# Sliding-window attention and a gated feed-forward layer: seven block products for eight in the last six tiles, with attention placed in the output stage

## The chip, the cores and the metric

The kernel runs on one core of one Trainium2 chip. Five engines of the core work from queues of their own, each in order: TensorE (PE; its weight loads are shown as PEld), VectorE (DVE), ScalarE (ACT), GpSimd (POOL) and SyncE (SP). They meet at semaphores. Results of TensorE land in PSUM, eight banks of 128 x 512 float32. The metric is the device time of one execution in microseconds.

## The reference

For each of 8 batches and 8 heads, queries, keys and values are 576 x 64. A query sees itself and the 63 keys before it:

```python
scores = scale * np.matmul(q, k.transpose(0, 1, 3, 2))
mask = (rel >= 0) & (rel < window)          # window = 64, rel = query - key
attn = softmax(np.where(mask, scores, -1e9))
x = (attn @ v).transpose(0, 2, 1, 3).reshape(B * S, H * D)     # 4608 tokens x 512
gate = np.maximum(x @ w_gate, 0.0)          # w_gate, w_val: 512 x 1536
val = x @ w_val
return (gate * val) @ w_out                 # w_out: 1536 x 512
```

## The kernel before

The 4608 tokens are cut into ten tiles: tiles 0 to 3 of 384 tokens (TT) and tiles 4 to 9 of 512 (WT), the wide ones. NS is 4. Matrix operands are float16, sums float32.

*Feed-forward part of a tile.* In the hidden stage (`hidden`, line 450 and on) the 1536 hidden features are 12 blocks of 128 (f), and the 512 inputs are 4 chunks of 128. For each f, four matmuls (L481) make the gate block in a PSUM bank, ScalarE applies the ReLU into `r_sb` (L466), four matmuls make the value block in another bank, and VectorE multiplies it by `r_sb` into `g_sb` (L469). The 12 `g_sb` blocks feed the output stage (`output`, `out_mm`, L495): for each 128 tokens, 12 matmuls of 512 columns, an evacuation by ScalarE (L502) and a DMA from SP.

*Attention of a tile.* q and k of a batch are loaded by DMA from the POOL queue (`qk_load`, L167) and transposed by VectorE in four instructions of 128 x 576 (`qk_trans`, L185). v is loaded by POOL's queue (`v_load`, L191) and partly copied to other partitions by POOL (`v_spread`, L200 and L202). A wide tile has two quads of four windows of 64 queries. For a quad, TensorE writes scores into four banks (`q_st`, L236), ScalarE takes the exponential (L365) and VectorE multiplies by the band mask (L369). Then TensorE multiplies by v (`t_pv`, L384), VectorE takes reciprocals of the sums (L399), normalises (L404) and transposes into `xt` (L409), the input of the hidden stage. Tiles 0 to 3 do the same in units of 192 tokens (L270, L275, L296, L310, L320, L340). While one tile is in its hidden and output stages, the attention of the next is placed among its matmuls.

*Order of the work.* The order in each queue is written by a planner, `Weaver`. Code that emits TensorE's main stream advances an estimated clock; other work is put into a heap with a due time (`W.at`) and is emitted, in order of due time, as soon as the clock passes it. Due times set only the order in each queue: an engine runs its next instruction when what it needs is there. `ahead(t)` plans at the beginning of tile t: for a wide tile the next tile's attention (`plan_wide`: scores, exponentials and masks, values) and k, q and v of the tile after that (`wide_loads`). A tile buffer drawn anew from a pool with n buffers waits until every use of the buffer n draws ago is over.

*Buffers.* PSUM is split into four single banks (`f_ps`, hidden and output stages, and a rest of the values) and two double banks (`a_ps`, scores and values). k and q landing buffers (`a_in`) are double.

Of the kernel before, what the change touches and what calls it, by code (L numbers as in the profile page):

```python
# [13 lines left out]
MUL = mybir.AluOpType.mult  # L14
ONE_ONE = struct.unpack("<f", struct.pack("<I", 0x3C003C00))[0]
# [29 lines left out]
def kernel(  # L45
# [20 lines left out]
    G = 4  # L66
# [11 lines left out]
    a_in = ctx.enter_context(tc.tile_pool(name="a_in", bufs=2))  # L78
    a_p = ctx.enter_context(tc.tile_pool(name="a_p", bufs=12))
    a_n = ctx.enter_context(tc.tile_pool(name="a_n", bufs=2))  # L80
    x_sb = ctx.enter_context(tc.tile_pool(name="x_sb", bufs=3))
    g_sb_p = ctx.enter_context(tc.tile_pool(name="g_sb", bufs=2))
    f_sb = ctx.enter_context(tc.tile_pool(name="f_sb", bufs=3))
    f_ps = ctx.enter_context(tc.tile_pool(name="f_ps", bufs=4, space=bass.MemoryType.PSUM))
    a_ps = ctx.enter_context(tc.tile_pool(name="a_ps", bufs=2, space=bass.MemoryType.PSUM))
# [3 lines left out]
    wo = persist.tile([128, NF, DM], FP16)  # L89
    qTs = [persist.tile([128, 2, S, 2], FP16, name=f"qT{i}") for i in range(2)]  # L90
# [72 lines left out]
    def qk_load(b, name, hh):  # L163

        tile_ = nat[b, name, hh] = a_in.tile([128, S // 32 * D], FP16, name=f"{name}{hh}", bufs=2)
        src = (q if name == "q" else k)[b, G * hh:G * hh + G]
        nc.gpsimd.dma_start(tile_, src.rearrange("h (i j) d -> (h i) (j d)", i=32))  # L167

    def first_load(name):

        t32 = nat["32", name] = x_sb.tile([128, S // 32 * D], FP32, name=f"{name}32", bufs=1)
        nc.sync.dma_start(t32, (q if name == "q" else k)[0, 0:G].rearrange("h (i j) d -> (h i) (j d)", i=32))

    def first_round(name, copies):
        n = S // 32 * D // len(copies)
        to = nat[0, name, 0] = a_in.tile([128, S // 32 * D], FP16, name=f"{name}0", bufs=2)
# [40 lines left out]
    def one_bank(name):  # L217
        return f_ps.tile([128, 512], FP32, name=name, tag="h")

    def two_banks(name):  # L220
        return a_ps.tile([128, 2, 512], FP32, name=name, tag="a")

    def st_tiles(u):
        d = units.setdefault(u, {})
        if u == 0:
            d["st"] = [one_bank("st") for _ in range(G)]
        else:
            halves = [two_banks("st") for _ in range(2)]
            d["st"] = [halves[g // 2][:, g % 2] for g in range(G)]
# [35 lines left out]
    def u_exp(u, i, hhs=(0, 1)):  # L265
        d = units[u]
        if d["p"][i] is None:
            d["p"][i] = a_p.tile([128, 2 * UB, 64], FP16, name="p")
# [10 lines left out]
    def u_pv(u, hhs=(0, 1), banks=None):  # L279

        d = units[u]
        if "pv" not in d:
            if banks:
                d["pv"] = [one_bank("pv") for _ in range(2)]
            else:
                both = two_banks("pv")
# [62 lines left out]
    wides = {}  # L349

# [3 lines left out]
    def q_st(qd):  # L354

        halves = [two_banks("st") for _ in range(2)]
        d = quads[qd] = {"st": [halves[g // 2][:, g % 2] for g in range(G)], "p": [None] * G}
# [4 lines left out]
    def q_exp(qd, g):  # L362
        d = quads[qd]
        d["p"][g] = a_p.tile([128, 2 * QW, 64], FP16, name="pw")
        nc.scalar.activation(d["p"][g].rearrange("p n c -> p (n c)"), d["st"][g], ACT.Exp, scale=scale)  # L365

    def q_mask(qd, g):
        p = quads[qd]["p"][g]
        nc.vector.tensor_tensor(p, p, mask[:, None, :].to_broadcast([128, 2 * QW, 64]), MUL)  # L369

    def t_pv(t):

        d = wides[t] = {"pv": [two_banks("pv") for _ in range(2)], "rest": one_bank("pv"),
                        "x": a_n.tile([128, 2, WS, 2, D // 2], FP16, name="xw"), "r": a_n.tile([128, 2, WS, 1], FP32, name="rw")}
        for qh in range(2):
            qd = 2 * (t - NS) + qh
            for hh in range(2):
                for i in range(QW):
                    b, vw = divmod(q_window(qd, i), NG)
                    for s in range(2):  # L380
                        n = 2 * (QW * qh + i) + s
                        to = d["pv"][hh][:, n // BS, VW * (n % BS):] if n < 2 * BS else d["rest"][:, VW * (2 * hh + n - 2 * BS):]
                        for j in range(G):
                            nc.tensor.matmul(to[32 * j:32 * j + 32, 0:D + 1],  # L384
                                             quads[qd]["p"][j][:, QW * hh + i, 32 * s:32 * s + 32],
                                             v16s[b % 2][:, vw, G * hh + j, 0:D + 1],
                                             start=True, stop=True, skip_group_check=True)
        return 1.25

    def t_parts(d, hh):  # L390

        rest = d["rest"][:, 0:4 * VW].rearrange("p (a s c) -> p a s c", a=2, c=VW)
        return [(d["pv"][hh][:, k, 0:BS * VW].rearrange("p (s c) -> p s c", c=VW), BS * k, BS * k + BS) for k in range(2)] + [
            (rest[:, hh], 2 * BS, WS)]

    def t_recip(t, hh):
        d = wides[t]
        for pv, s0, s1 in t_parts(d, hh):
            nc.vector.reciprocal(d["r"][:, hh, s0:s1], pv[:, :, D:D + 1])  # L399

    def t_norm(t, hh, k):
        d = wides[t]
        pv, s0, s1 = t_parts(d, hh)[k]
        nc.vector.tensor_tensor(d["x"][:, hh, s0:s1], pv[:, :, 0:D].rearrange("p s (c e) -> p s e c", e=2),  # L404
                                d["r"][:, hh, s0:s1, :, None].to_broadcast([128, s1 - s0, 2, D // 2]), MUL)

    def t_turn(t, hh):
        dst = xt_tile(t)[:, 2 * hh:2 * hh + 2].rearrange("p e (s c) -> p s e c", c=32)
        nc.vector.transpose(dst, wides[t]["x"][:, hh])  # L409
        if hh == 1:  # L410
            normed[0] = t

    def plan_wide(t, TA, TB, P):
        for qd, T in ((2 * (t - NS), TA), (2 * (t - NS) + 1, TB)):
            W.at(T, lambda qd=qd: q_st(qd))
            for g in range(G):
                W.at(T + 0.8 + 0.55 * g, lambda qd=qd, g=g: q_exp(qd, g))
                W.at(T + 1.35 + 0.55 * g, lambda qd=qd, g=g: q_mask(qd, g))
# [301 lines left out]
```

## Time and profile before

| quantity | value |
|---|---|
| three runs | 324.62 us each |
| span of the profiled execution | 323.2 us; its own time is not listed, so 1.4 us around it are taken from the runs |
| PE busy | 312.2 us, 97% |
| DVE busy | 191.7 us, 59% |
| ACT busy | 128.9 us, 40% |
| POOL busy | 95.2 us, 29% |
| granted TensorE clock | 1.000 |
| tile 2, from 68.06 us | 25.68 us |
| tile 3, from 93.74 us | 26.15 us |
| tile 4, from 119.89 us | 33.89 us |
| tiles 5 to 8 | 33.86 us each where shown |

Busy time on PE includes the modelled tail of each matmul, so its share does not tell how near TensorE is to its peak. The start of a matmul minus the start of the one before it is its price in a stream. Idle time of an engine that does not set the end costs nothing. In an answer of the profile, a line gives line number, engine, operation, output and inputs with their shapes, a count after x, and busy time with the mean of one; the idle time before it and what ended it stand at the end. In the chain and the timelines the first two numbers are start and length in us.

### The profile page before, as it was taken

The page shows a single profiled execution, that of the slowest core. Times are in us where ns is not written, and L with a number is a line of the kernel's source. Part 1 is how long each engine was busy: PE and PEld are TensorE (multiplying, and loading weights), DVE is VectorE, ACT ScalarE, POOL GpSimd, SP SyncE. Part 2 cuts the span into 40 slices and gives each one's busy share as a digit, 9 for nine tenths or more (in the row PEclk, how much of TensorE's full clock was granted, in tenths as well). Part 3 has the DMA queues.
Part 4 walks back from the last instruction along what each step waited for, and adds up shares of the span by engine and source line. Part 5 has one row for each costly group of instructions (what it writes and reads, how often), then busy time and mean ns, then how long its engine had stood idle before and what let it go on. Part 6 is the DMA issues. An engine that isn't in the chain of part 4 may idle for free.

```text
span 323.2 us, 8917 instructions
## 1 busy us (share of the span) xinstructions
PE 312.2 (97%) x3861; PEld 167.7 (52%) x3861; DVE 191.7 (59%) x367; ACT 128.9 (40%) x256; POOL 95.2 (29%) x140
## 2 busy tenths in 40 slices
PE   4689999999999999999999999999999999999996
PEld 2466958656556644454445444454445444544444
DVE  5937962677938759564765656673767145724410
ACT  3545325534434623542354234613371337223322
POOL 8759317284910290029100920072000000000000
PEclk9999999999999999999999999999999999999999
DMA  7999997979294079009910893092000200020002
GB/s 214 182 190 199 179 143 173 157 127 184 35 203 60 9 95 202 3 5 122 218 10 2 108 203 27 2 103 88 0 3 34 99 0 2 5 110 20 0 34 98
DMA packets 52488, 29.48 MB, mean 91 GB/s; under 512 B 38880, under 2 KB 43872, under 8 KB 52448
## 3 DMA queue, kind: packets, MB, share of 16 engines
q0 software_dynamic: 46688, 18.29, 48.8%
q1 hardware_dynamic: 5616, 10.55, 9.0%
q8 instruction: 30, 0.49, 0.6%
q14 instruction: 10, 0.08, 0.1%
q10 hardware_dynamic: 144, 0.07, 0.1%
HBM read 37.75 MB, written 9.44 MB: 146 GB/s over the span
## 4 chain that ended last, share of the span: by engine, by line
PE 94%; DMA 2%; POOL 1%; DVE 1%; issue 1%; ACT 0%; DVEq 0%; POOLq 0%
PE h L481 59%; PE op L495 28%; PE st L236 3%; PE pv L384 2%; DMA v<-in_v_dram 2%; PE pv L296 1%; PE op L527 1%; DVE x L320 0%; POOL v L191 0%; DVE v L202 0%; POOL k L167 0%; DVE v L200 0%; POOL q L167 0%; DVE xt L340 0%; POOL ident L107 0%
## 5 line engine op out<-in xcount | busy, mean ns | idle before, releaser
L469 DVE TENSOR_TENSOR g_sb<-r_sb,h 128x512 f16<-128x512 f32 (+1 forms) x120 | 75.4, 631 | 88.5 <-PE h L481 86.8
L481 PE MATMUL h<-xt,wg 128*128 128x512 f16 (+2 forms) x544 | 111.8, 335 | 1.5 <-issue 0.9
L481 PE MATMUL h<-xt,wv 128*128 128x512 f16 (+2 forms) x544 | 111.4, 335 | 0.0
L466 ACT ACTIVATE r_sb<-h 128x512 f32<-128x512 f32 (+1 forms) x120 | 66.8, 558 | 89.1 <-PE h L481 81.3
L495 PE MATMUL op<-wo,g_sb 128*128 128x512 f16 x420 | 93.8, 379 | 0.0
L481 PEld LDWEIGHTS <-wg 128*128 128x128 f16 x544 | 50.8, 98 | 43.9 <-issue 2.0
L481 PEld LDWEIGHTS <-wv 128*128 128x128 f16 x544 | 50.4, 98 | 40.9
L495 PEld LDWEIGHTS <-g_sb 128*128 128x128 f16 x420 | 40.4, 98 | 47.1
L191 POOL DMA_DIRECT2D v<-in_v_dram x41 | 34.6, 864 | 94.0 <-PE pv L384 89.2
L502 ACT COPY o_sb<-op 128x512 f32<-128x512 f32 x35 | 20.5, 586 | 85.9 <-PE op L495 85.2
L369 DVE TENSOR_TENSOR pw<-pw,mask 128x512 f16<-128x512 f16 x48 | 19.2, 422 | 14.6 <-ACT pw L365 14.3
L365 ACT ACTIVATE pw<-st 128x512 f16<-128x512 f32 x48 | 25.7, 605 | 5.0 <-PE st L236 4.5
L200 POOL COPY v<-v 64x512 f16<-64x512 f16 (+1 forms) x22 | 16.0, 728 | 27.1 <-DMA v<-in_v_dram 26.3
L185 DVE STREAM_TRANSPOSE kT<-k 128x576 f32<-128x576 f32 x16 | 20.0, 1247 | 0.1
L185 DVE STREAM_TRANSPOSE qT<-q 128x576 f32<-128x576 f32 x16 | 19.3, 1238 | 0.1
L202 POOL COPY v<-v 64x512 f16<-64x512 f16 (+1 forms) x22 | 17.0, 771 | 1.0
L404 DVE TENSOR_TENSOR xw<-pv,rw 128x448 f16<-128x448 f32 (+1 forms) x36 | 16.2, 507 | 0.4
L236 PEld LDWEIGHTS <-kT 32*128 32x128 f16 x1152 | 10.6, 92 | 9.3 <-issue 7.7
L270 ACT ACTIVATE p<-st 128x384 f16<-128x384 f32 (+1 forms) x40 | 13.8, 439 | 3.8 <-PE st L236 3.7
L409 DVE STREAM_TRANSPOSE xt<-xw 128x1024 f16<-128x1024 f16 x12 | 14.9, 1244 | 0.4
L236 PE MATMUL st<-qT,kT 32*128 32x64 f16 x1152 | 12.6, 190 | 1.6 <-DVE qT L185 1.6
L275 DVE TENSOR_TENSOR p<-p,mask 128x384 f16<-128x384 f16 x24 | 10.2, 456 | 3.4 <-ACT p L270 3.3
(49 smaller groups left out, 98.2 us busy)
## 6 DMA issues: line engine op xcount, KB each, us to landing
out_dram<-o_sb SPq DMA_DIRECT2D x35, 256.0 KB, 2.8
k<-in_k_dram POOLq DMA_DIRECT2D x15, 288.0 KB, 5.7
q<-in_q_dram POOLq DMA_DIRECT2D x15, 288.0 KB, 8.3
v<-in_v_dram POOLq DMA_DIRECT2D x31, 128.0 KB, 9.1
wg<-in_moe_w_gate_dram POOLq DMA_DIRECT2D x6, 256.0 KB, 6.6
wv<-in_moe_w_val_dram POOLq DMA_DIRECT2D x6, 256.0 KB, 8.4
wo<-in_moe_w_out_dram POOLq DMA_DIRECT2D x3, 512.0 KB, 12.8
v<-in_v_dram POOLq DMA_DIRECT2D x10, 64.0 KB, 6.1
```

Of the source, the lines that this page charges most:

```text
L185: nc.vector.transpose(dst.rearrange("p (i j) -> p j i", i=32)[:, j0:j1], src[:, j0:j1])
L191: nc.gpsimd.dma_start(v16s[b % 2][lo:hi, g, :, 0:64], v[b, :, 64 * g - 64 + lo:64 * g - 64 + hi].rearrange("h p d -> p h d"))
L202: copy(t[0:64, g0:g1:2, h0:h1, 0:64], t[64:128, g0 - 1:g1 - 1:2, h0:h1, 0:64])
L236: return [lambda dh=dh: nc.tensor.matmul(to, kTs[b % 2][rows, hh, 64 * w:64 * w + 128, dh], qTs[b % 2][rows, hh, 64 * w:64 * w + 64, dh], ...
L365: nc.scalar.activation(d["p"][g].rearrange("p n c -> p (n c)"), d["st"][g], ACT.Exp, scale=scale)
L369: nc.vector.tensor_tensor(p, p, mask[:, None, :].to_broadcast([128, 2 * QW, 64]), MUL)
L404: nc.vector.tensor_tensor(d["x"][:, hh, s0:s1], pv[:, :, 0:D].rearrange("p s (c e) -> p s e c", e=2), d["r"][:, hh, s0:s1, :, None].to_bro ...
L466: nc.scalar.activation(part(r_sb), part(h1), ACT.Relu)
L469: nc.vector.tensor_tensor(g_sb[:, f:f + w, c0:c0 + n], part(r_sb), part(h2), MUL)
L481: nc.tensor.matmul(h[:, b * n:b * n + n], wt[:, c, (f + b) * 128:(f + b) * 128 + 128], xt[:, c, c0:c0 + n], start=(c == 0), stop=(c == NC ...
L495: nc.tensor.matmul(op, g_sb[:, f, bass.ds(sub * 128, 128)], wo[:, f], start=(f == 0), stop=(f == NF - 1))
L502: nc.scalar.copy(o_sb, op)
```

## The change

In tiles 4 to 9, x @ w_val is computed block-wise. The 512 inputs, the 1536 features and the 512 tokens are each cut in two, which gives four weight blocks and four input blocks. Seven products of combined blocks replace the eight of the plain way (in the diff: P1 to P7; one product is four matmuls of 256 columns for 2 x 128 features). The weight combinations (`vs`, `w_form`) are made once, on POOL, during tile 2. The input combinations (`xc`, `x_form`) are made per tile, on VectorE. P1, P6, P7 and P4 accumulate in one PSUM bank A; ScalarE copies A to SBUF after the first three (`snap`). B takes P2, C takes P5 and later P3. VectorE adds copies to B and C (`add`), and the gating product of three results is made by POOL from SBUF, that of the fourth (`direct`) by VectorE from A. Gate blocks, four per group, stand between the products.

The attention of wide tiles moves: during the output stage of tile t, before its four output blocks, stand the two value halves of tile t + 1 and the two score quads of tile t + 2 (`fast_output`, `between`). Tile 3 carries the scores of tiles 4 and 5 and the values of tile 4. k and q transposes of a batch are due in four slots of the hidden stage (`SLOTS`), and v copies at spaced times. PSUM becomes a list of free banks for tiles 4 to 9 (`bank`), `a_in` becomes single, and tiles 1 to 3 run their hidden stage four gate blocks and four value blocks at a time (`each=4`, `r4`).

```diff
+    a_in = ctx.enter_context(tc.tile_pool(name="a_in", bufs=1))
...
-    x_sb = ctx.enter_context(tc.tile_pool(name="x_sb", bufs=3))
+    x_sb = ctx.enter_context(tc.tile_pool(name="x_sb", bufs=4))
...
-    f_ps = ctx.enter_context(tc.tile_pool(name="f_ps", bufs=4, space=bass.MemoryType.PSUM))
-    a_ps = ctx.enter_context(tc.tile_pool(name="a_ps", bufs=2, space=bass.MemoryType.PSUM))
+    psum = ctx.enter_context(tc.tile_pool(name="psum", bufs=1, space=bass.MemoryType.PSUM))
+    singles = [psum.tile([128, 512], FP32, name=f"bank{i}") for i in range(4)]
+    doubles = [psum.tile([128, 2, 512], FP32, name=f"banks{i}") for i in range(2)]
...
+    vs = persist.tile([128, 4, 2, 128 * HF], FP16)
...
+    free = []
+
+    def bank():
+
+        while not free:
+            W.pop()
+        return free.pop(0)
+
+    def read(to, give):
+        unread.discard(id(to))
+        if give:
+            free.append(to)
...
+    def x_form(t, n):
+
+        if t not in xcs:
+            xcs[t] = x_sb.tile([128, 4, 2, HT], FP16, name="xc", tag="xt")
+        xt, xc = xt_tile(t), xcs[t]
+        b11, b12, b21, b22 = (xt[:, 2 * k:2 * k + 2, HT * h:HT * h + HT] for k in range(2) for h in range(2))
+        x, y = ((b12, b11), (b22, xc[:, 0]), (b22, b12), (b21, xc[:, 1]))[n]
+        nc.vector.tensor_tensor(xc[:, n], x, y, SUB)
+        if n == 3:
             normed[0] = t
...
+    def values(t, hh, T, banks=None):
+
+        t_pv(t, hh, banks or [bank() for _ in range(3)], banks is None)
+        W.clock += 0.62
+        W.at(T + 0.7, lambda: t_recip(t, hh))
+        for i, k in enumerate((2, 0, 1)):
+            W.at(T + 1.2 + 0.5 * i, lambda k=k: t_norm(t, hh, k))
+        W.at(T + 2.7, lambda: t_turn(t, hh))
+        for n in ((0,), (1, 2, 3))[hh]:
+            W.at(T + 4.0 + 0.4 * n, lambda n=n: x_form(t, n))
+
+    def w_form(n, j):
+
+        c = slice(256 * j, 256 * j + 256)
+        f = slice(256 * j + 128 * HF, 256 * j + 128 * HF + 256)
+        a11, a12, a21, a22 = wv[:, 0:2, c], wv[:, 2:4, c], wv[:, 0:2, f], wv[:, 2:4, f]
+        x, y, op = ((a21, a22, ADD), (vs[:, 0, :, c], a11, SUB), (a11, a21, SUB), (a12, vs[:, 1, :, c], SUB))[n]
+        nc.gpsimd.tensor_tensor(vs[:, n, :, c], x, y, op)
...
+            r4 = f_sb.tile([128, 4, WT], FP32, name="r4", bufs=2)
...
+                    h = one_bank()
...
-                        r_sb = r_sbs[c0, f] = f_sb.tile([128, WT], FP32, name="r_sb", bufs=6)
+                        r_sb = r_sbs[c0, f] = r4[:, len(r_sbs)]
...
+    def fast_hidden(t):
+
...
+        def group(j):
...
+            forms = {"P1": (wv[:, 0:2, c], b11), "P2": (wv[:, 2:4, c], b21), "P3": (vs[:, 3, :, c], b22),
+                     "P4": (wv[:, 2:4, f], xc[:, 3]), "P5": (vs[:, 0, :, c], xc[:, 0]),
+                     "P6": (vs[:, 1, :, c], xc[:, 1]), "P7": (vs[:, 2, :, c], xc[:, 2])}
+
+            def product(name, to, first):
+                W.advance(W.clock)
+                if first:
+                    at[to] = bank()
+                w, x = forms[name]
+                for i in range(2):
+                    for k in range(2):
+                        nc.tensor.matmul(at[to][:, HT * i:HT * i + HT], w[:, k, 128 * i:128 * i + 128], x[:, k],
+                                         start=(first and i == 0 and k == 0), stop=(k == 1), skip_group_check=True)
+                W.clock += 4 * (HT + 7) / 2400.0
...
+            def snap(name):
+                def copy():
+                    at[name] = f_sb.tile([128, 512], FP32, name="snap", bufs=5)
+                    nc.scalar.copy(at[name], at["A"])
+                W.at(W.clock, copy)
+
+            def add(delay, to, name, last, n, h):
+
+                def summed():
+                    v = f_sb.tile([128, 512], FP32, name="vsum", bufs=4)
+                    nc.vector.tensor_tensor(v, at[to], at[name], ADD)
+                    at["summed", n, h] = True
+                    if last:
+                        free.append(at[to])
+
+                    def mult():
+                        nc.gpsimd.tensor_tensor(gh[:, 2 * j + HF * n:2 * j + HF * n + 2, h], rh[:, 2 * n:2 * n + 2, h], pair(v), MUL)
+                        done[2 * j + HF * n, h] = done[2 * j + HF * n + 1, h] = True
+                    W.at(max(W.clock, at["relus", n]) + 0.7, mult)
+                W.at(W.clock + delay, summed)
...
+            def direct():
+                def mult():
+                    nc.vector.tensor_tensor(gh[:, 2 * j + HF:2 * j + HF + 2, 0], rh[:, 2:4, 0], pair(at["A"]), MUL)
+                    free.append(at["A"])
+                    done[2 * j + HF, 0] = done[2 * j + HF + 1, 0] = True
+                W.at(W.clock + 0.2, mult)
+
+            T = W.clock
+            at["relus", 1], at["relus", 0] = T + 3.7, T + 6.8
+            product("P1", "A", True)
+            snap("a1")
+            gate(2)
+            product("P6", "A", False)
+            snap("u2")
+            product("P2", "B", True)
+            add(0.1, "B", "a1", True, 0, 0)
+            gate(3)
+            product("P5", "C", True)
+            product("P7", "A", False)
+            snap("u3")
+            add(0.8, "C", "u3", False, 1, 1)
+            gate(0)
+            product("P4", "A", False)
+            direct()
+            gate(1)
+            while ("summed", 1, 1) not in at:
+                W.pop()
+            product("P3", "C", False)
+            add(0.1, "C", "u2", True, 0, 1)
...
+    F_LAST = [f for j in range(NF // 4) for f in (2 * j + HF, 2 * j + HF + 1, 2 * j, 2 * j + 1)]
+
+    def fast_output(t, between):
+
+        g_sb, done = gs[t]
+        for sub, before in enumerate(between):
+            for fn in before:
+                fn()
+            op = bank()
+            for i, f in enumerate(F_LAST):
+                if i % 4 == 0:
+                    W.advance(W.clock)
+                while (f, sub // 2) not in done:
...
-        def wide_loads(t, T):
+        L_T = 3 * 6.53
+        WIDE_T = L_T + 13.1
...
+        def qk_ahead(t, T, gaps):
+            b, new = batch_of(t)
+            if new:
+                plan_batch(b, T - 12.0, [T + x for x in gaps])
...
+        def v_ahead(t, T):
...
+            for i, u in enumerate(us):
+                W.at(T - 5.0, lambda u=u: v_load(u))
+                W.at(T + 6.0 + 2.5 * i, lambda u=u: v_spread(u, pool))
...
+        LAST = NS + NL - 1
+        SLOTS = (2.6, 6.53 + 0.8, 6.53 + 2.6, 2 * 6.53 + 0.8)
...
+            if t == NS - 2:
+                qk_ahead(NS, T + 28.5, (0.0, 1.4, 2.8, 4.2))
+                v_ahead(NS, T + 27.0)
+                for j in range(NF // 4):
+                    for n, at in enumerate((0, 1, 3, 2)):
+                        W.at(T + 2.0 + 6.0 * j + 1.4 * n, lambda at=at, j=j: w_form(at, j))
...
+            if t == NS - 1:
+                qk_ahead(NS + 1, T + 12.0, (0.0, 1.4, 2.8, 4.2))
+                for qd, x in ((0, 9.5), (1, 12.8), (2, 19.0), (3, 22.3)):
+                    def st(qd=qd):
+                        scores(qd, W.clock, [half for _ in range(2) for half in halves_of[id(two_banks())]], qd == 3)
+                    W.at(T + x, st)
+                for hh in range(2):
+                    def pv(hh=hh):
+                        values(NS, hh, W.clock, halves_of[id(two_banks())] + [one_bank()])
+                    W.at(T + 16.2 + 0.1 * hh, pv)
+                qk_ahead(NS + 2, T + 24.5, SLOTS)
+                v_ahead(NS + 1, T + 24.5)
+            if NS <= t:
+                if t + 3 <= LAST:
+                    qk_ahead(t + 3, T + WIDE_T, SLOTS)
+                if t + 2 <= LAST:
+                    v_ahead(t + 2, T + WIDE_T)
 
         W.at(15.0, lambda: loads(3, 70.0))
...
-        hidden(1, ((U, TT),))
+        hidden(1, ((U, TT),), each=4)
         output(1)
-        for t in range(2, NS + NL):
+        for t in range(2, NS):
             ready(t)
             ahead(t)
-            hidden(t, ((0, widths[t]),))
-            (output if t < NS + NL - 1 else output_last)(t)
+            hidden(t, ((0, widths[t]),), each=4)
+            output(t)
+        W.advance(W.clock)
+        while any(id(one) in unread for one in singles):
+            W.pop()
+        free.extend(singles[(taken["one"] + i) % 4] for i in range(4))
+        for t in range(NS, NS + NL):
+            ready(t)
+            ahead(t)
+            fast_hidden(t)
+            between = [[] for _ in range(4)]
+            if t + 1 <= LAST:
+                between[0].append(lambda: values(t + 1, 0, W.clock))
+                between[1].append(lambda: values(t + 1, 1, W.clock))
+            if t + 2 <= LAST:
+                for qh in range(2):
+                    between[2 + qh].append(lambda qh=qh: scores(2 * (t + 2 - NS) + qh, W.clock))
+            if t == LAST:
+                fast_output(t, between[:-1])
+                W.drain()
+                output_last(t)
+            else:
+                fast_output(t, between)
```

## The prediction

> **What bounds the kernel now.** I read the chain of waits first, its pieces in order of time second, the groups kept apart by shape third, and the timelines of single engines last.
>
> ```profile
> PE 94%; DMA 2%; POOL 1%; DVE 1%; issue 1%; ACT 0%; DVEq 0%; POOLq 0%
> ```
>
> ```profile
> 93.74 9.75 PE h L481 x60
> 103.49 0.62 PE st L236 x60
> 104.11 2.71 PE h L481 x16
> 106.81 0.62 PE st L236 x62
> 107.43 2.71 PE h L481 x16
> 110.14 1.23 PE pv L384 x123
> ...
> 119.89 12.09 PE h L481 x56
> ```
>
> TensorE carries the end: from 17.6 us on the pieces follow each other without a hole. A wide tile lasts 33.86 us (119.89, 153.78, 187.64, ...). So TensorE work taken away counts in full, and any wait put on TensorE counts in full too. The first five lines are tile 3: hidden stage, with two score blocks in it, then the value block at 110.14.
>
> ```profile
> 317.44 1.47 PE L527 MATMUL op<-wo,g_sb 128*128 128x256 f16 x12
> ```
>
> ```profile
> 127.70 0.60 ACT L466 ACTIVATE r_sb<-h 128x512 f32<-128x512 f32 x1 [1.08 <-PE h L481]
> ```
>
> ```profile
> 60.16 1.50 DVE L275 TENSOR_TENSOR p<-p,mask 128x384 f16<-128x384 f16 x4 [0.35 <-ACT p L270]
> ...
> 80.92 2.37 DVE L275 TENSOR_TENSOR p<-p,mask 128x384 f16<-128x384 f16 x3
> ...
> 96.92 1.25 DVE L185 STREAM_TRANSPOSE kT<-k 128x576 f32<-128x576 f32 x1
> 98.02 0.54 DVE L469 TENSOR_TENSOR g_sb<-r_sb,h 128x384 f16<-128x384 f32 x1
> 98.48 1.22 DVE L185 STREAM_TRANSPOSE kT<-k 128x576 f32<-128x576 f32 x1
> ...
> 110.07 0.42 DVE L369 TENSOR_TENSOR pw<-pw,mask 128x512 f16<-128x512 f16 x1
> 111.08 0.58 DVE L399 RECIPROCAL rw<-pv 128x7 f32<-128x7 f32 x3 [0.60 <-PE pv L384]
> 111.70 1.35 DVE L404 TENSOR_TENSOR xw<-pv,rw 128x128 f16<-128x128 f32 x3
> 112.97 0.54 DVE L469 TENSOR_TENSOR g_sb<-r_sb,h 128x384 f16<-128x384 f32 x1
> 113.43 1.23 DVE L409 STREAM_TRANSPOSE xt<-xw 128x1024 f16<-128x1024 f16 x1
> ```
>
> These are VectorE's start-to-start prices: transpose 1.07 to 1.10, gate product 0.46, mask 0.34, three normalisations 1.27. In tile 3 its last mask ends at 110.49, after TensorE has already begun the value block at 110.14. VectorE has little to spare there.
>
> **The change, part by part.** The sum is made against the profiled span of 323.2 us. The three runs are all 324.62, so 1.4 us lies around the span and I carry it unchanged.
>
> *Seven products for eight.* A 512-column matmul costs 12.09/56 = 0.216 us. A 256-column one costs (1.47 - 0.27)/11 = 0.109 us, its weight load hidden. Four blocks of w_val cost 16 x 0.216 = 3.45 us now and 7 x 4 x 0.109 = 3.06 after. That is 0.40 saved in each of 3 groups in 6 tiles: **-7.1 us**. The gate products stay. A group then lasts 3.06 + 3.45 = 6.51 us.
>
> *Partial sums.* Bank A is copied by ScalarE between two products. After P1 and after P7 one gate block (0.864 us) separates the last matmul from the next write into A. Counted from the start of that last matmul, the write is due 0.109 + 0.864 = 0.973 later. A 256-column matmul ends after 0.273. ScalarE starts 0.04 after a matmul's modelled end (last gate matmul 127.285 + 0.379, relu 127.70), its PSUM copy takes 0.586 (the output copies), and TensorE starts 0.05 after a releaser (transpose before 14.86). Together 0.95, so 0.02 is left: cost **0**, but with no cover. VectorE starts 0.11 after the same kind of end when two engines release it; at that price each hand-off misses by 0.05, and 36 of them cost 1.8. A gain is excluded, since nothing waits there now. The bounds are 0 and +1.8. I take 0, since a relu is the same engine and kind as the copy. The third copy (after P6) has 1.7 us. ScalarE then has seven 0.6 us instructions in 6.5.
>
> *VectorE and POOL in a group.* Three additions and one product, each shaped like the gate product (0.686), replace four gate products; 2.7 of 6.5 us. The sum out of C must be read before P3: about 1.6 us after P7's slot against 2.17, hidden. k/q transposes fall into the 1.5 us gaps. POOL gets three two-input products per group. No row shows one. The nearest is its one-input copy, 0.61 for 64x512, 1.04 for 64x1024; I bound it by 0.6 and 2.1 (two such reads) and take 1.04, the row with as many elements read. Cover: the first output block needs the last group's h=0 product 2.2 us after the stage begins, plus a value block of 0.6. Two products follow P7's sum, so a price up to about 1.8 is hidden; at 2.1 the stage waits 0.6 in five tiles and 1.2 in the last, +4. The Trainium skill, GPSIMD Engine Reference, section 3.1, gives 4497 ns for 2048 elements, an estimate of 1.1 us here; with it the sum is the same.
>
> *Attention moved into the output stage.* Score and value blocks cost the same (0.62, 1.23), but values are split in two; each break costs about 0.09, five more breaks: **+0.45**. In a 13.1 us output stage VectorE has 6.5 (reciprocals, normalisations, transposes) + 1.4 (four subtractions at the mask's price) + 2.7 (masks); the next hidden stage's xc is done some 4 us early. Hidden. The p, bank and r4 buffers come free earlier than they are asked for. v loads wait on POOL for the value block, as at 143.49 now, but that is done before they reach the queue's head; k/q loads find their transposes a stage behind. Output DMAs on SP are as before.
>
> *Weight sums on POOL in tile 2.* Twelve, about 12 us at 1.04. They stand in the queue behind v copies that wait for DMA until 78 us or earlier, and move the next k/q loads from 65.7 to about 77. Those are needed at 92: hidden by 6 us. If POOL needed 2.1 each, they would land near 97: up to +3.
>
> *Groups of four in tiles 1 to 3.* In tile 2, transposes due at 3.7 and 5.1 after the stage's start now run among the four gate products. The fourth ends at 7.5, and its bank is asked for at 7.15: **+0.4** (0 if the transposes come a little earlier, 1.1 if one more gets ahead).
>
> *Tile 3 takes a second attention.* It now also hosts tile 5's scores (two 0.62 blocks, moved, no net cost), tile 4's xc, and four more k/q transposes (due 12.0 to 16.2 after its start) that did not run here. Times from its start: the last gate product before the scores' masks ends at 11.8. From then VectorE has, in queue order, 8 masks (2.7), 4 transposes (4.3) and 2 gate products (0.9): 7.9, so the last mask ends near 19.8. TensorE is at the value block at 16.4, does the half that needs only the first quad (0.62), and waits from 17.0 to 19.9: **+2.9**. The v copies of POOL, now queued behind k/q loads that wait for the earlier transposes, run at about 9.6 to 14.2, beside four of these masks. Beside POOL copies three masks took 2.37, alone four took 1.50: about +0.3 for two or three of them, **+0.65**. Then the scores of tile 5 need the value banks back: TensorE reaches them 1.5 us after the value block (0.65 + 0.87), VectorE needs one gate product, six reciprocals, six normalisations and another gate product, to about 24.1 against 22.05: **+2.1**. Afterwards TensorE has 8 us of work, VectorE 4.5. Bounds for the three together: 2 if the transposes slide behind the masks' waits, 8 if the k/q data, loaded only when the old tiles are free, arrive 2 us late.
>
> Sum: -7.1 + 0.45 + 0.4 + 2.9 + 0.65 + 2.1 = -0.6, or **-0.7** with the products unrounded (-7.14). 324.6 - 0.7 = **323.9 us**.
>
> **The rivals.**
> 1. *VectorE keeps up in tile 3.* For: its mean load there is 18.67 us in 26.15 now. Against: the work is bunched between the scores and the value block. With waits of 2 or less for 5.65, and tile 2's 0.4 gone: 319.9 to 320.5; with half the waits 321.1.
> 2. *The snapshots miss (slower).* One mechanism: ScalarE's copy out of A ends after its gate block. It decides when a hand-off misses by more than 0.06 us (36 x 0.06 = 2.2). For: 0.02 of slack; ScalarE also has relus in its queue. Against: its relus start 0.04 after their matmul. At 0.1 us each: 323.9 + 3.6 = 327.5.
> 3. *TensorE slows after the tile 3 waits (slower).* The first eight 384-column matmuls (4.35 us, cold start) run 0.31 apart, later ones 0.16. If the wait of 3.5 us brings that pace back, each us of work then takes two: 2 us of work behind each wait costs 2, or 4 for both: 326 to 328. Against: idle stretches of 1.4 us before 14.9 bring no second slow run. The Trainium skill, TensorE: Matmul & The Clock Gate, Part 1, puts the window at about 3.4 us of idleness; by that rule the first wait is at the edge and the second below it, so 1.7 more once. No run here shows it yet.
> 4. *The change does not do what it says*, because a 256-column matmul runs at the weight load's pace (0.098 mean): excluded, 0.109 is measured with loads.
>
> **How the numbers follow.** Forecast case 0.45, own range 322.6 to 325.2. Rival 1 0.25, rival 2 0.15, rival 3 and a slow POOL together 0.15. Leaving out a tenth each side: 320.0 to 327.5. A measurement of this kernel tells 0.2% (0.65 us) from no change: below 323.97 is faster. The forecast case gives half of its chance to faster (0.23), 0.17 to same and 0.05 to slower; rival 1 all to faster; 2 and 3 to slower. Faster 0.48, same 0.17, slower 0.35.
>
> **What would show it.** Products in the timeline 0.109 apart and wide tiles of 32.8 us confirm the gain. A TensorE wait of about 3 us on mask L369's successor before tile 4's value block, and one of 2 us on the normalisation before the following scores, confirm tile 3. Waits of TensorE on ScalarE's copy confirm rival 2; 256- or 512-column matmuls at double pitch after a hole confirm rival 3. The forecast is wrong if tile 3 has no such holes, or if the wide tiles are not 1.1 us shorter.

## The result and the profile after

The changed kernel took **346.02 us** in the median (345.63 to 346.55, four runs) beside 324.62 us for the kernel before: a ratio of 1.0663, interval 1.0648 to 1.0678. The forecast was 323.9 us and its range ended at 327.5, so the result lies 18.5 us beyond the range, on the slow side. The profiled execution has a span of 344.3 us (346.27 us in all), 21.1 us more than before.

The first two parts of the profile after, TensorE's row and the granted clock, and the engines' shares of the chain of waits:

```profile
PE 314.6 (91%) x4077; PEld 189.5 (55%) x4077; DVE 201.1 (58%) x391; ACT 158.5 (46%) x310; POOL 176.9 (51%) x206
...
PEclk9999999999999899999999999999999999999999
...
PE 27%; ACT 2%; DVE 1%; issue 1%; ACTq 0%; DVEq 0%
```

TensorE's share fell from 97% to 91%, while ScalarE, VectorE and POOL stay far from full, and the clock is lower in one slice only. So no engine became the bound: TensorE waits. The chain is followed back only to 234.94 us here, so its shares do not add up to the span. What it does show is new: ScalarE now has 2% where it had 0%.

The waits of TensorE after, from tile 3 on (columns: total us, times, longest), with those below 1 us in total left out:

```profile
PE banks L579 <- ACT r L592: 4.3, 10, 0.7
PE banks L664 <- ACT pw L395: 2.7, 4, 0.7
PE banks L588 <- ACT snap L599: 2.5, 4, 0.8
PE banks L428 <- DVE pw L400: 2.5, 3, 1.2
PE banks L579 <- ACT snap L599: 1.9, 3, 0.8
PE banks L664 <- ACT o_sb L669: 1.9, 2, 1.2
```

One of the six was forecast: the value block that waits for masks (L428 on L400, tile 3). The others have two things in common. The tile about to be written is `banks`, never `bank`, and the instruction that ends the wait belongs to another block: a product (L579) waits for the ReLU of a gate block, a gate block (L588) for a snapshot of A, an output block (L664) for an exponential.

Summed over the trace (start-to-start distances of successive matmuls beyond their undisturbed 0.216 us at 512 columns and 0.109 at 256), TensorE loses 22.4 us from tile 4's start at 126.29 to the end. Some 20 us of them, in 30 stops of 0.18 to 1.02 us, stand before writes into `banks` that begin when ScalarE or VectorE has just finished with a `banks` tile (in some of these A itself is such a tile, and a few tenths may be its own hand-off). In the kernel before the same count is 1.4 us from 126 us on.

One such place, first on TensorE, then on ScalarE:

```profile
245.45 0.60 PE L579 MATMUL banks<-xc,vs 128*128 128x256 f16 x4
246.83 0.60 PE L579 MATMUL banks<-xt,wv 128*128 128x256 f16 x4 [0.79 <-ACT snap L599]
...
245.71 0.60 ACT L592 ACTIVATE r<-banks 128x512 f32<-128x512 f32 x1 [0.34 <-PE banks L588]
246.20 0.58 ACT L599 COPY snap<-banks 128x512 f32<-128x512 f32 x1
```

The first product is P6 into A, whose snapshot ScalarE copies from 246.20 to 246.78. The second is P2 into B. B cannot be A, which still collects P7 and P4. Yet P2 starts at 246.83, 0.05 after the copy of A, and in the trace its first matmul waits for ScalarE's semaphore.

The reason stands in two lines of the change:

```diff
+    doubles = [psum.tile([128, 2, 512], FP32, name=f"banks{i}") for i in range(2)]
+    halves_of = {id(two): [two[:, i] for i in range(2)] for two in doubles}
```

Four of the eight entries in the free list are halves of two double tiles. The reading at this point: a wait is written for the whole tile, so a write into one half waits for the reader of the other half. Before, both halves of a double tile belonged to the same attention step, so this cost nothing.

Stage by stage, in us (predicted values as the prediction's text adds up: tile 3 is 26.15, two moved score blocks of 0.62, and 5.65 of waits):

| stage | before | predicted | after |
|---|---|---|---|
| tile 2 | 25.68 | 26.1 | 26.12 |
| tile 3 | 26.15 | 33.0 | 32.79 |
| tile 4 | 33.89 | 32.8 | 37.25 |
| tile 5 | 33.86 | 32.8 | 36.16 |
| tile 4 to the end | 203.3 | | 218.0 |

Tiles 2 and 3 came out at the forecast times (tile 3 partly by luck, as the last part on the sum shows). What made the kernel slower is in the wide tiles.

### The profile page after: what moved, and what is told of

It reads as the page before. It is cut to its first block, busy times and chain, and to the rows that moved or that the text cites. A ratio compares the mean times of both kernels' runs of the same rounds, so it can differ in the third digit from the quotient of the medians.

```text
span 344.3 us, 9467 instructions
## 1 busy us (share of the span) xinstructions
PE 314.6 (91%) x4077; PEld 189.5 (55%) x4077; DVE 201.1 (58%) x391; ACT 158.5 (46%) x310; POOL 176.9 (51%) x206
## 5 line engine op out<-in xcount | busy, mean ns | idle before, releaser
L612 POOL TENSOR_TENSOR g_sb<-r,vsum 128x512 f16<-128x512 f32 x54 | 67.9, 1272 | 105.9 <-DVE vsum L606 102.8
L664 PEld LDWEIGHTS <-g_sb 128*128 128x128 f16 x276 | 25.6, 98 | 36.7 <-issue 8.7
L664 PE MATMUL banks<-wo,g_sb 128*128 128x512 f16 x168 | 39.6, 379 | 6.5 <-ACT pw L395 2.7
L588 PE MATMUL banks<-xt,wg 128*128 128x512 f16 x160 | 41.0, 379 | 2.9 <-ACT snap L599 2.5
L588 PEld LDWEIGHTS <-wg 128*128 128x128 f16 x288 | 28.1, 98 | 22.5 <-issue 3.9
L531 DVE TENSOR_TENSOR g_sb<-r,bank 128x384 f16<-128x384 f32 x48 | 25.8, 549 | 23.0 <-PE bank L544 21.7
L579 PEld LDWEIGHTS <-vs 128*128 128x128 f16 x288 | 28.1, 97 | 18.9 <-issue 5.2
L544 PE MATMUL bank<-xt,wg 128*128 128x192 f16 (+1 forms) x256 | 34.8, 286 | 1.2 <-DVE xt L358 0.6
L592 ACT ACTIVATE r<-banks 128x512 f32<-128x512 f32 x40 | 23.8, 597 | 24.6 <-PE banks L588 22.3
L544 PE MATMUL bank<-xt,wv 128*128 128x192 f16 (+1 forms) x256 | 34.4, 286 | 0.0
L679 PE MATMUL bank<-wo,g_sb 128*128 128x512 f16 x144 | 34.1, 389 | 0.0
L588 PE MATMUL bank<-xt,wg 128*128 128x512 f16 x128 | 32.9, 379 | 0.0
L400 DVE TENSOR_TENSOR pw<-pw,mask 128x512 f16<-128x512 f16 x48 | 20.5, 438 | 13.8 <-ACT pw L395 12.8
L579 PEld LDWEIGHTS <-wv 128*128 128x128 f16 x216 | 21.0, 97 | 13.5 <-issue 6.1
L592 ACT ACTIVATE r<-bank 128x512 f32<-128x512 f32 x32 | 19.1, 598 | 18.2 <-PE bank L588 18.2
L210 POOL COPY v<-v 64x512 f16<-64x512 f16 (+1 forms) x22 | 16.0, 726 | 22.4 <-DMA v<-in_v_dram 21.4
```

What stands on the lines that cost most here:

```text
L400: nc.vector.tensor_tensor(d["p"][g], d["p"][g], mask[:, None, :].to_broadcast([128, 2 * QW, 64]), MUL)
L531: nc.vector.tensor_tensor(g_sb[:, f:f + w, c0:c0 + n], part(r_sb), part(h2), MUL)
L544: nc.tensor.matmul(h[:, b * n:b * n + n], wt[:, c, (f + b) * 128:(f + b) * 128 + 128], xt[:, c, c0:c0 + n], start=(c == 0), stop=(c == NC ...
L579: nc.tensor.matmul(at[to][:, HT * i:HT * i + HT], w[:, k, 128 * i:128 * i + 128], x[:, k], start=(first and i == 0 and k == 0), stop=(k == ...
L588: nc.tensor.matmul(to, wg[:, k, 128 * ff:128 * ff + 128], xt[:, k], start=(k == 0), stop=(k == NC - 1))
L592: nc.scalar.activation(r4[:, n], to, ACT.Relu)
```

## The experiments

Times of one group of runs are from one chip, with the kernel before at 324.60 us (323.84 to 324.85, thirteen runs); the last two kernels ran on another chip, with the kernel before at 324.27 us (323.73 to 324.88, nine runs).

### Eight banks as eight tiles

The two double tiles become four tiles of one bank. Nothing else is changed but what this needs (two reciprocals in place of one on a double).

```diff
-    doubles = [psum.tile([128, 2, 512], FP32, name=f"banks{i}") for i in range(2)]
-    halves_of = {id(two): [two[:, i] for i in range(2)] for two in doubles}
+    doubles = [[psum.tile([128, 512], FP32, name=f"part{i}{j}") for j in range(2)] for i in range(2)]
+    halves_of = {id(two): two for two in doubles}
...
-            d["st"] = [halves[g // 2][:, g % 2] for g in range(G)]
+            d["st"] = [halves[g // 2][g % 2] for g in range(G)]
...
-            nc.vector.reciprocal(d["r"], d["both"][:, :, 0:SB * VW].rearrange("p a (s c) -> p a s c", c=VW)[:, :, :, D:D + 1])
+            for hh in hhs:
+                nc.vector.reciprocal(d["r"][:, hh], pv_of(d, u, hh)[:, :, D:D + 1])
```

> The changed kernel with its two double-bank tiles replaced by four single-bank ones, so that all eight PSUM banks are tiles of their own; nothing else moves. In the changed kernel's trace TensorE stands still for 22.4 us from 126 us on, 20.6 of them before a matmul into a half of a double tile, ended by a reader of a double tile. Theory (a reader of one half holds up a write into the other half, because the two halves are one tile): these waits go, about 20 us in all; time 325 to 327 us, wide tiles near 32.8 us, and what is left are hand-offs of some 0.03 us after a snapshot. Rival (ScalarE, with seven 0.6 us instructions per 6.5 us group, is simply too late): the waits stay under other bank names, above 10 us, and the time stays above 335 us.

Measured: **324.84 us** (323.01 to 325.37, ten runs), ratio 1.000, interval 0.9983 to 1.0018. The whole 21.2 us are gone with the double tiles, and the time is just under the 325 to 327 that were expected. TensorE's waits of 0.4 us or more:

```profile
PE bank L223 <- DVE bias L126: 4.4, 1, 4.4
PE part L428 <- DVE pw L400: 2.5, 3, 1.2
PE bank L544 <- DVE xt L358: 1.0, 2, 0.5
PE bank L544 <- DVE g_sb L531: 0.4, 1, 0.4
PE part L579 <- ACT snap L599: 0.4, 1, 0.4
```

Every wait of an L579, L588 or L664 matmul on a foreign reader has left the list; one L579 wait is left, and that one is on A's own snapshot. From tile 4 on TensorE now loses 2.56 us by the same count, against 22.4. The wide tiles last 33.39, 33.08, 32.91 and 32.87 us (32.8 predicted). TensorE writes one bank while ScalarE reads another, without a stall, so it was no limit of the memory either. The Trainium skill, PSUM — Partial Sum Buffer, The four PSUM rules, rule 1, says that each bank is a separate physical SRAM; this run agrees. The wait was written by the program, per tile.

### One double tile kept

The same kernel, with one of the two pairs still a double tile: two shared halves among the eight banks, for four in the changed kernel.

```diff
-    doubles = [[psum.tile([128, 512], FP32, name=f"part{i}{j}") for j in range(2)] for i in range(2)]
+    whole = psum.tile([128, 2, 512], FP32, name="banks0")
+
+    def pair_of(i):
+        return [psum.tile([128, 512], FP32, name=f"part{i}{j}") if i else whole[:, j] for j in range(2)]
+
+    doubles = [pair_of(i) for i in range(2)]
```

> As the run with eight single-bank tiles, but one of the two double tiles is kept, its halves still one tile. Theory (halves of one tile): less than half of the waits remain, since only one pair of eight banks can collide where two could; 5 to 10 us of waits, time 330 to 336 us, and all long waits are before writes into the pair that was kept. Rival (ScalarE too late): the time is that of the changed kernel, 346 us, within 2.

Measured: **337.63 us** (336.82 to 339.09, four runs), ratio 1.0413, interval 1.0384 to 1.0443. One pair costs 12.8 us over eight single banks, two pairs 21.2. The direction is as expected and 337.6 lies above the range given, so one pair costs more than half of two. Its largest waits from tile 3 on (the added lines shift each line number by 5: L592 is L597, L599 is L604, L664 is L669):

```profile
PE banks L584 <- ACT r L597: 2.8, 6, 0.7
PE banks L593 <- ACT snap L604: 2.5, 4, 0.8
PE part L433 <- DVE pw L405: 2.5, 3, 1.2
PE banks L669 <- ACT pw L400: 1.4, 2, 0.7
PE banks L669 <- DVE vsum L611: 0.9, 1, 0.9
```

All but the forecast mask wait are on the one pair that is left (`banks`); the two banks of the pair that was split (`part`) show no such wait. That the price does not go with the number of pairs fits the mechanism: what a write waits for depends on which user happens to hold the other half, and the order of hand-outs shifts with every change. The runs do not show more than that.

### The products put back to plain ones

Eight single banks, and in tiles 4 to 9 plain value blocks again: four 512-column matmuls, gated by VectorE. The input and weight combinations are still made and not used, so that VectorE's and POOL's load before the products stays; the snapshots, the sums and POOL's gating products are left out.

```diff
+    def plain_hidden(t):
...
+        for fb in range(0, NF, 4):
+            r4 = f_sb.tile([128, 4, WT], FP32, name="r4", bufs=2)
+            for n in range(4):
+                f = F_LAST[fb + n]
...
+                for wt in (wg, wv):
...
+                        nc.tensor.matmul(h, wt[:, c, 128 * f:128 * f + 128], xt[:, c], start=(c == 0), stop=(c == NC - 1))
...
+                def mult(f=f, n=n, h=hs[1], r4=r4):
+                    nc.vector.tensor_tensor(g_sb[:, f], r4[:, n], h, MUL)
...
-            fast_hidden(t)
+            plain_hidden(t)
```

> Eight single-bank tiles and attention in the output stage, but the value blocks of the last six tiles are the plain eight products of 512 columns, gated by VectorE; the weight and input combinations are still made and not used. Theory (seven products for eight save TensorE 7.1 us and their hand-offs cost next to nothing once the false waits are gone): 6 to 7.5 us slower than the run with eight single-bank tiles, 331 to 334 us. Rival (hand-offs through ScalarE eat the gain): within 2 us of that run.

Measured: **330.98 us** (329.69 to 331.38, four runs), ratio 1.0207, interval 1.019 to 1.0224. The seven products are worth 6.1 us of the median. The profiled run of this kernel had the full granted clock (329.69 us); the two runs of the eight-bank kernel at full clock took 323.01 and 323.04, which is 6.7 apart at equal clock. From tile 4 to the end, where both traces have the full clock, the plain products take 202.9 us and the seven products 196.7: 6.2. Predicted were 7.14 for the products less what the snapshots cost (below, 0.86), 6.3. So the saving is real and of the size worked out; the double tiles buried it.

### Tile 3 planned anew

Eight single banks, and other due times in tiles 2 and 3: the scores of tile 4 and the four k/q transposes earlier, the values earlier.

```diff
-                qk_ahead(NS, T + 28.5, (0.0, 1.4, 2.8, 4.2))
+                qk_ahead(NS, T + 24.5, (0.0, 0.3, 0.6, 0.9))
...
-                qk_ahead(NS + 1, T + 12.0, (0.0, 1.4, 2.8, 4.2))
-                for qd, x in ((0, 9.5), (1, 12.8), (2, 19.0), (3, 22.3)):
+                qk_ahead(NS + 1, T + 12.0, (-3.5, -2.1, -0.7, 0.7))
+                for qd, x in ((0, 5.3), (1, 8.6), (2, 18.0), (3, 21.3)):
...
-                    W.at(T + 16.2 + 0.1 * hh, pv)
+                    W.at(T + 14.0 + 0.1 * hh, pv)
```

> Eight single-bank tiles, and tile 3's attention planned anew: tile 4's k/q transposes come at the end of tile 2, tile 3's score blocks 4 us earlier, tile 5's transposes 3.5 us earlier, the value block 2.2 us earlier. Theory (in tile 3 the value block waits about 2.5 us for the last mask behind four added transposes, and then TensorE runs at half pace for 2 us): both losses go, tile 3 lasts 28 to 29.5 us in place of 32.8, and the time is 3 to 4.5 us below the run with eight single-bank tiles: 321 to 323. Rival (VectorE has no room in tile 3 at all): the wait moves to the scores of tile 5 or to tile 4's first combined product, and the time is within 1 us of that run.

Measured: **322.54 us** (321.88 to 323.29, four runs), ratio 0.9944, interval 0.9923 to 0.9965: faster than both kernels. Tile 3 lasts 30.25 us for 32.95, where 28 to 29.5 were expected. What was left of the holes, on TensorE's timeline:

```profile
104.82 0.66 PE L254 MATMUL part<-qT,kT 32*128 32x64 f16 x61 [0.30 <-ACT pw L395]
...
112.55 0.24 PE L428 MATMUL bank<-v,pw 128*32 128x65 f16 x8 [0.64 <-DVE g_sb L531]
...
117.14 0.20 PE L254 MATMUL part<-qT,kT 32*128 32x64 f16 x2 [0.21 <-DVE xw L447]
117.67 0.66 PE L254 MATMUL part<-qT,kT 32*128 32x64 f16 x61 [0.33 <-DVE xw L447]
```

The long wait for masks is gone, and three shorter ones have come: at score quad 1 (the exponential that frees its banks), in the value block (a gate product that frees a bank), and at score quad 2 (normalisations that free the value banks). They cost about 0.7, 0.8 and 0.9 us.

Part of what was gained is the clock. In the eight-bank kernel's trace TensorE's granted clock is 0.50 for 3.41 us inside tile 3 (116.15 to 119.56), which costs 1.7 of the 2.70 us by which the tile differs; in the replanned kernel's trace it is 1.00 there. The waits themselves are then about 1.0 us shorter, and so are the runs at full clock (322.25 and 321.88 us, beside 323.01 and 323.04 with eight banks).

### The left holes, moved

On top of that, the places with holes later, and the four transposes of tile 2 together before its first gate product. The kernel replanned above ran again beside it.

```diff
-                    plan_batch(b, T - 12.0, (T, T + 1.4, T + 2.8, T + 4.2))
+                    plan_batch(b, T - 12.0, (T, T + 0.2, T + 0.4, T + 0.6))
...
-                for qd, x in ((0, 5.3), (1, 8.6), (2, 18.0), (3, 21.3)):
+                for qd, x in ((0, 5.3), (1, 9.6), (2, 19.3), (3, 22.3)):
...
-                    W.at(T + 14.0 + 0.1 * hh, pv)
+                    W.at(T + 15.2 + 0.1 * hh, pv)
```

> On top of e3_replan: the four k/q transposes of tile 2 are due together before its first gate product, score quad 1 of tile 3 one microsecond later, the value block 1.2 later, the last two score quads 1.3 and 1.0 later. Theory (the holes that e3_replan keeps are places where the written order asks VectorE or ScalarE too early, so a later place closes them): in e3_replan TensorE stood 0.37 us in tile 2 before its fifth value block, about 0.7 at score quad 1, 0.8 at the value block, 0.9 at score quad 2, 2.8 in all. If two thirds of it close: 322.5 - 1.9 = 320.6 us, tile 2 at 25.8 and tile 3 near 29.0 (30.25 in e3_replan). Rival (the work that VectorE must do between those places is the limit, so holes only move to the next place): tile 3 stays at 29.8 to 30.5 and only the 0.37 of tile 2 goes: 322.0 to 322.5 us.

> The same kernel as e3_replan, beside e5_holes on the same chip, so that a difference of 0.4 to 2 us can be told: 322.5 us, tile 3 at 30.25.

Measured: **320.45 us** (319.95 to 321.25, five runs), ratio 0.9886, interval 0.9866 to 0.9905; the replanned kernel beside it 322.46 us (322.18 to 322.85), ratio 0.9944, interval 0.9931 to 0.9957. The 2.0 us between them were expected as 1.9. TensorE in tile 2, and the two holes of tile 3 that are left:

```profile
72.43 2.76 PE L544 MATMUL bank<-xt,wg 128*128 128x384 f16 x16
75.03 2.76 PE L544 MATMUL bank<-xt,wv 128*128 128x384 f16 x16
...
107.32 0.81 PE L544 MATMUL bank<-xt,wg 128*128 128x384 f16 x4 [0.42 <-DVE g_sb L531]
...
111.73 0.24 PE L428 MATMUL bank<-v,pw 128*32 128x65 f16 x8 [0.44 <-DVE g_sb L531]
```

Tile 2 has no hole and lasts 25.62 us; tile 3 lasts 29.06 (29.0 expected). The hole of tile 2 stood, by the row at 75.67 in the replanned kernel's trace, before the eighth gate block and not before a value block, as the expectation has it; the cure is the same. So most of VectorE's work fits, and it was mainly the order that was wrong: of the holes in tile 3 two of 0.42 and 0.44 us are left. This is the best version: 3.8 us faster than the median before beside it (324.27 us), where the change as made was 21.4 us slower than its own 324.62.

## Why the prediction was wrong, point by point

**The step that failed** is the sentence "The p, bank and r4 buffers come free earlier than they are asked for", within the part on attention in the output stage. It counted when each bank's own reader is done. It did not ask in which unit a wait is kept. With eight single banks it holds: no foreign wait is left. With two double tiles it cost 21.2 us, shown by undoing that part alone, and 12.8 us with one double. No rival covered it, and the trace of before could not show it, since there the halves of a double always had one user; but the diff did: four of the entries that `bank` hands out are slices of two tiles. The cost to bound was the reader's time, about 0.6 us, at each of the many hand-outs from `doubles`. One such wait in each of the 18 groups is 10.8 us, past the end of the range.

**The rest of the sum** can be read in the kernel with eight single banks, which came to 324.84 us (323.0 in the two runs at full clock) where the sum said 323.9.

- *Products, -7.1:* right, as the plain products show (6.1 us in the median, 6.7 at equal clock, 6.2 in the traces from tile 4 on, with the snapshots' own cost inside).
- *Snapshot hand-off, 0, bounds 0 to 1.8:* 0.86 us. Most of it, 0.51, is one place, the first group of tile 4. Eight-bank kernel, TensorE, then ScalarE:

```profile
126.95 1.03 PE L588 MATMUL bank<-xt,wg 128*128 128x512 f16 x4
128.33 0.60 PE L579 MATMUL part<-xc,vs 128*128 128x256 f16 x4 [0.35 <-ACT snap L599]
...
126.72 0.59 ACT L686 COPY o_sb<-bank 128x512 f32<-128x512 f32 x1 [0.51 <-PE bank L679]
127.20 0.60 ACT L395 ACTIVATE pw<-part 128x512 f16<-128x512 f32 x1
127.69 0.59 ACT L599 COPY snap<-part 128x512 f32<-128x512 f32 x1
```

The copy of A starts at 127.69, behind an output copy and an exponential in ScalarE's queue, and P6 waits for it. This is what rival 2 named, ScalarE's other work in the queue; elsewhere the slack of 0.02 us held or missed by 0.07. Rival 2 as a whole needed a miss at each of the 36 hand-offs and did not come.
- *Breaks in the output stage, +0.45:* right. Each break costs 0.09 to 0.10 us in the eight-bank kernel too, and there are five more.
- *Groups of four in tile 2, +0.4:* right. In the kernel after, the fourth gate bank of the next four is late:

```profile
75.06 0.81 PE L544 MATMUL bank<-xt,wg 128*128 128x384 f16 x4 [0.37 <-DVE g_sb L531]
```

- *Tile 3's wait for the last masks, +2.9, and POOL beside them, +0.65:* right in size, partly by luck. TensorE in the kernel after:

```profile
111.81 0.70 PE L428 MATMUL banks<-v,pw 128*32 128x65 f16 x65
113.16 0.20 PE L428 MATMUL banks<-v,pw 128*32 128x65 f16 x1 [0.65 <-DVE pw L400]
113.95 0.20 PE L428 MATMUL banks<-v,pw 128*32 128x65 f16 x1 [0.59 <-DVE pw L400]
115.37 0.51 PE L428 MATMUL banks<-v,pw 128*32 128x65 f16 x21 [1.22 <-DVE pw L400]
...
116.36 4.12 PE L679 MATMUL bank<-wo,g_sb 128*128 128x512 f16 x13
```

  From 111.81 to 116.36 are 4.55 us for a block of 1.23: 3.3 lost, 3.55 predicted. But both ends of this wait came about 2 us later than was worked out, and so cancel: TensorE reached the block 18.3 us after the tile's start for 16.4, and VectorE's last mask ended at 21.8 for 19.8. VectorE had four gate products among the masks where two were counted, and POOL's copies (103.34 to 108.27) made the first masks dearer by more than 0.65. VectorE, two masks beside these copies and the next two:

```profile
105.36 1.78 DVE L400 TENSOR_TENSOR pw<-pw,mask 128x512 f16<-128x512 f16 x2
...
108.16 0.73 DVE L400 TENSOR_TENSOR pw<-pw,mask 128x512 f16<-128x512 f16 x2
```
- *Score banks wanted back, +2.1:* wrong, it did not come. The step placed the next scores 1.5 us after the value block; the planner had put 13 output matmuls between (the last line above, 2.8 us at full pace), in which VectorE caught up. That half pace stretched these 13 matmuls is not the reason: with plain products they ran at full pace, the scores came at 119.01, and the list of that kernel's waits has none there. In the replanned kernel this wait does appear (117.14 and 117.67, on the normalisation), though the scores come 4.0 us after the value block. There the last gate products stand behind the value block, and two of them (113.66 and 114.95) delay the reciprocals and the large normalisations, the order that the step had assumed.
- *Rival 3, half pace after the tile 3 waits:* partly true. Those 13 matmuls took 4.12 us where 2.98 is the undisturbed figure (below); six stand about 0.43 apart, so +1.15 us here and +1.7 in the eight-bank kernel, against 2 or 4 for two waits by rows. The 1.7 once that rival 3 worked out from the Trainium skill, TensorE: Matmul & The Clock Gate, Part 1, fits these runs. The argument against, that idle stretches before 14.9 us bring no second slow run, did not hold; the longest there behind the start is 1.11 us. So tile 3 was right in its sum, 32.79 for 33.0, by luck: the 2.1 us for the score banks did not come, and in their place stand half pace (1.15) and a wait of the second score block for exponentials (about 0.45, at 107.86), which had no term.
- *POOL's share, hidden:* right, though each product is dearer than the 1.04 taken and than the estimate of 1.1 beside it. The page's group of the gating products after, and one of the weight combinations with shapes kept apart:

```profile
L612 POOL TENSOR_TENSOR g_sb<-r,vsum 128x512 f16<-128x512 f32 x54 | 67.9, 1272 | 105.9 <-DVE vsum L606 102.8
```

```profile
L486 POOL TENSOR_TENSOR vs<-wv 128x512 f16<-128x512 f16 x6 | 6.9, 1162 | 0.1
```

  1.27 us is below the 1.8 at which the output stage would wait, and none of the output blocks of the eight-bank kernel waits for POOL. The k loads of the next batch start at 75.45 (about 77 predicted).

## What to carry over

When buffers are handed out from a free list, each entry should be one unit of the dependency tracking: a slice of a larger tile makes two unrelated users wait for each other. In a diff that loosens an order, ask of every buffer not only when its reader is done but which other readers share its name. A list of TensorE's waits in which the releaser has no business with the waiting line is the sign to look for; and once that was repaired, a late VectorE was largely cured here by moving due times alone (2.3 us, of which about 1.0 at equal clock, and then 2.0).

## What the runs showed of the hardware beyond what was expected

Half pace does not need one unbroken idle stretch, and it is not the same in each run. In tile 3 the three idle stretches before it (0.65, 0.59 and 1.22 us beside the matmuls' modelled tails) were cut by a single small matmul each. With these same stretches the 13 output matmuls behind took 4.12 us in the kernel after, 4.67 with eight banks, and 2.98 with plain products, where no matmul was slow:

```profile
113.26 0.20 PE L428 MATMUL part<-v,pw 128*32 128x65 f16 x1 [0.65 <-DVE pw L400]
114.06 0.20 PE L428 MATMUL part<-v,pw 128*32 128x65 f16 x1 [0.60 <-DVE pw L400]
115.48 0.35 PE L428 MATMUL part<-v,pw 128*32 128x65 f16 x21 [1.22 <-DVE pw L400]
...
116.10 2.98 PE L707 MATMUL bank<-wo,g_sb 128*128 128x512 f16 x13
```

The granted clock tells where the difference comes from. In the traces of the kernel after and of the one with eight banks it falls to 0.50 for one stretch of 3.41 us and is 1.00 before and after. Within each trace the times between two changes of the clock are whole multiples of 3.413 us (31 of them before this stretch in the kernel after, 60 behind it with eight banks). So the clock changes on a grid, and the grid lies elsewhere in each execution. The stretches of the grid around the holes:

| kernel | stretch | TensorE busy in it | granted clock in the next stretch |
|---|---|---|---|
| after | 111.89 to 115.31 | 1.03 us | 0.50 (to 118.72) |
| eight banks | 112.73 to 116.15 | 1.11 us | 0.50 (to 119.56) |
| plain products | 110.77 to 114.18 | 2.17 us | 1.00 |
| plain products | 114.18 to 117.60 | 2.20 us | 1.00 |

(With plain products the clock does not change here; the stretches are counted on from the first record of that trace's clock.) In the kernel after, half the clock was granted from 1.05 us before the 13 matmuls on, so less of it fell on them than with eight banks, where it began with them. With plain products the holes were divided between two stretches, and no half clock followed. So with the same holes 0 to 1.7 us hang on where the grid falls. How little work in a stretch is too little stays open: near the start of the replanned kernel 1.95 us of it (11.16 to 14.58) were followed by half the clock, and 1.92 us in the kernel with the holes moved (12.29 to 15.71) were not.

The Trainium skill, TensorE: Matmul & The Clock Gate, Part 1, says that the window in which the clock's control watches TensorE runs freely; these traces agree.

It shows in the runs too: of the ten with eight banks, two have a granted clock of 1.000 and took 323.01 and 323.04 us, the other eight have 0.989 to 0.995 and took 324.38 to 325.37. One half-clock stretch costs 1.7 us and brings the mean clock to 0.995; where it lay in the runs without a trace is not shown. With the long wait planned away the profiled runs of tile 3 hold full pace.
